# An attention and Fourier kernel whose planner leaves one PSUM bank free: scores borrow banks only while one stays, and the order's keys are spaced anew

## The chip, the cores and the metric

The kernel runs on one core of one Trainium2 chip. The metric is the time of one execution in device microseconds (us). Of the kernel before there are three timed runs, of which the median counts, and one more execution under the profiler.

## The reference, cut to what matters

Two sublayers over 2048 tokens of width 448, with their outputs side by side in one array of 2048 x 896:

```
a = einsum("bsd,ed->bse", x, dft_hid_re);  b = einsum("bsd,ed->bse", x, dft_hid_im)
y = einsum("ts,bse->bte", dft_seq_re, a) - einsum("ts,bse->bte", dft_seq_im, b)      # A: Fourier mixing
...
q, k, v = the 16 heads of x @ wqkv, 28 wide each                                        # B: attention
p = softmax(einsum("bhqd,bhkd->bhqk", q, k) * 28 ** -0.5)
out = concat_heads(einsum("bhqk,bhkd->bhqd", p, v)) @ wo
return concatenate([y, out], axis=-1)
```

All inputs and outputs are fp32.

## The kernel before, in words

**The numbers.** TensorE (PE in the profile) takes its operands as fp32r. To keep precision, most operands are split into a high part (a copy, by ScalarE) and a low part (the rest, by VectorE), and a product is a sum of two or three matmuls: high by high, low by high, high by low.

**The two kinds of PE work.** The first is attention, in `head_once` (line 1156) and `score` (line 1127). For each of 16 heads there are 16 tiles of 128 keys and 4 chunks of 512 queries, so 64 scores, 1024 in all. A *score* is one matmul at L1130 of 85 rows (the split operands and a row with the maximum to subtract) into one bank of PSUM. ScalarE (ACT) reads the bank, takes the exponential and writes it to a tile `kept` in SBUF (L1134); then the bank is free again. After 16 scores a *weighting* follows (`four`, L1141): 16 products of the exponentials by the values, 32 columns wide and four side by side, each recorded as two matmuls. There are 64 weightings. Behind each head (for the last head, behind each chunk) `normal` (line 1188) copies the sums out (L1194), sends them through DRAM to form reciprocals and stores the head's output to `on_d`.

The second kind is called *fill* here, since it stands in the order wherever scores leave room: the projections to q, k and v and the transform over the width (helper `chain`, L571), the transform over the tokens with its rows halved by symmetry (`sequence_halved`, L901, with matmuls of 448 or 226 columns), one middle row (L849), and the output projection (`project_late`: L1364, and its last rows L1395). Fill chains accumulate into one bank over 9 to 12 matmuls or, in `sequence_halved`, over a chunk of many. A few small matmuls (L1114) find the maxima of 32 keys per head (`tops`).

**The banks of PSUM.** There are eight. Four (`fill_s`, in the order's names bank_270 to bank_273) are for fill, four (`bank_s`, bank_274 to bank_277) for scores, weightings and `tops`. The pool of the scores has the pool of fill as its lender: when none of its own is free, it takes one of the lender's (line 381, and `Slots.can_take` and `Slots.take`, lines 117 to 130).

**What sets the order.** Every instruction is a task with a key. `Schedule.run` plays the tasks through on guessed durations: for each engine it takes, among the tasks that are ready and whose buffers are free, the one with the smallest key; the sequence that comes out is what each engine's queue gets. On the chip each engine then runs its queue strictly in that order, and waits by semaphores where something isn't there yet. Fill gets its keys by `fkey` (line 470), spaced evenly up to `T_FILL`; head h's scores start at `T_ATT + h * (T_END - T_ATT) / H` (line 455) and follow each other at `DT`; the output rows' last step has keys from `T_OUT`. The numbers are the planner's microseconds, and only their order counts. A weighting goes first when PE has just done one and another is ready, and it is preferred by its key otherwise.

A second path, for inputs whose checks (`flag`, L1423) fail, lies behind a branch and isn't executed in the profile.

Of the kernel before, what the change touches and what calls it, by code (L numbers as in the profile page):

```python
# [35 lines left out]
NQS = 8  # L36
NQB = 1
NFILL = 4
NQ = 4
QT = NT // NQ  # L40
Q_YO = 2
# [57 lines left out]
class Slots:  # L99
# [17 lines left out]
    def can_take(self, slots, before):  # L117
        n = sum(since <= before for _, since in self.free)
        if self.lender:
            n += sum(since <= before for _, since in self.lender.free)  # L120
        if n < len(slots) + max(s.spare for s in slots):
            return False
        if self.in_turn:
            return all(s in self.turns[:n] for s in slots)
        return True
# [187 lines left out]
def tile_kernel(ctx, tc, xa, wre, wim, wd, xb, wqkv, wo, out):  # L313
# [8 lines left out]
    def new(name, shape, dtype=F32, n=None, in_turn=False):  # L322
        if n is None:
            return sb.tile(shape, dtype, tag=name, name=name)
        sch.pools.append(Slots([sb.tile(shape, dtype, tag=f"{name}{i}", name=f"{name}{i}") for i in range(n)], in_turn))
        return sch.pools[-1]
# [10 lines left out]
    mid_d = dram.tile([1, D], F32, name="midd")  # L337
    far_d = [dram.tile([P, D], F32, name=f"fard{n}") for n in range(2 * NQ)]

# [23 lines left out]
    ones = new("ones", [P, 1])  # L363
    diff = new("diff", [P, 2 * NQ + 1, 3 * QT + 1])
    whole = new("whole", [P, 2 * NQ + 1])
    alike = new("alike", [P, 2, 2 * NQ + 1])
    edge = new("edge", [P, 4, NT])
# [12 lines left out]
    sch.pools.append(raw_s)  # L380
    fill_s, bank_s = Slots(banks[:NFILL]), Slots(banks[NFILL:])
    bank_s.lender = fill_s
# [5 lines left out]
    nc.gpsimd.memset(diff[:, :, 3 * QT:], 0.0)  # L388
    nc.gpsimd.memset(diff[:, 2 * NQ, 4:3 * QT], 0.0)
    nc.vector.tensor_tensor(fold, ident[:, :VW], ident[:, VW:2 * VW], op=ALU.add)  # L390
# [47 lines left out]
            nc.vector.tensor_copy(dst, src)  # L438


    T_ATT, T_END, T_FILL, T_OUT = 34.0, 755.0, 824.0, 766.0
    units = [(h, c) for h in range(H - 1) for c in range(NC)] + [(H - 1, c) for c in LAST]
    due, head_due, head_due_b = {}, {}, {}

# [578 lines left out]
    before = {}  # L1023
# [462 lines left out]
```

## Time and profile before

| | |
|---|---|
| median of three runs | 865.23 us (864.64 to 870.12) |
| the profiled execution, its own time | 868.95 us |
| its span, first to last instruction | 866.7 us |
| granted TensorE clock, mean over the span | 0.98 |
| PE busy, matmuls | 843.5 us, 97% of the span |
| ScalarE busy | 634.9 us, 73% |
| VectorE busy | 375.6 us, 43% |
| first score, last score start (trace) | 65 us, 825 us |

How to read it: "PE" rows are matmuls, "PEld" the loads of their stationary operand, which overlap. A row's start is when the matmul was taken up, and its duration reaches to its modelled end. Since matmuls overlap in the pipeline, the time that one costs is the distance from its start to the next start, not its duration, and PE counts as busy while it in fact waits a fraction of a microsecond between two of them. The timeline merges neighbours of one kind: "x16" is sixteen in a row. In the table by windows each engine has its busy time and the number of its instructions, followed by the granted clock (1.00 is full), the share of the DMA engines and GB/s.

### The profile page before, as it was taken

What the parts mean: (1) busy time and instruction counts of PE and PEld (TensorE: products, weight loads), DVE (VectorE), ACT (ScalarE), POOL (GpSimd) and SP (SyncE); (2) the same over time, 40 slices, a digit from 0 to 9 for tenths busy, and PEclk for the clock granted to TensorE, in tenths of its full rate; (3) what the DMA queues carried; (4) which work ended last, traced back from release to release, by engine and by line L of the source; (5) the groups of instructions that cost most, each with busy time, mean ns of one, the idle gap of its engine ahead of it and who ended that gap; (6) DMA issues with size and microseconds to landing.
All of it is one profiled execution on the core that took longest, in us unless ns stands there. A gap on an engine that the chain in (4) does not pass through costs nothing.

```text
span 866.7 us, 14119 instructions
## 1 busy us (share of the span) xinstructions
PE 843.5 (97%) x4856; PEld 532.5 (61%) x4856; DVE 375.6 (43%) x888; ACT 634.9 (73%) x1287; POOL 6.0 (1%) x27
## 2 busy tenths in 40 slices
PE   8988999999999999999999999999999999999896
PEld 7875455556555556666556655667566656666575
DVE  7541013111311132222379463667766575756341
ACT  6107787787877878878899766789887876788831
POOL 2000000000000000000000000000000000000000
PEclk9998999999999999999989999999899999999999
DMA  9867634424343454434597664558886653746433
GB/s 285 207 113 192 193 116 123 158 90 133 100 152 111 127 155 122 132 112 142 172 219 220 204 189 137 179 171 246 192 250 208 191 171 119 224 144 175 125 117 106
DMA packets 156239, 141.27 MB, mean 163 GB/s; under 512 B 69310, under 2 KB 125120, under 8 KB 156160
## 3 DMA queue, kind: packets, MB, share of 16 engines
q1 hardware_dynamic: 156160, 140.29, 54.9%
q8 instruction: 40, 0.66, 0.3%
q14 instruction: 39, 0.32, 0.1%
HBM read 98.82 MB, written 43.12 MB: 164 GB/s over the span
## 4 chain that ended last, share of the span: by engine, by line
PE 86%; ACT 5%; DMA 4%; DVE 2%; SPq 1%; issue 1%; ACTq 0%; DVEq 0%
PE bank L1130 27%; PE bank L1141 25%; PE bank L571 18%; PE bank L901 10%; ACT kept L1134 3%; PE bank L1364 3%; DMA wraw<-wre 1%; PE bank L849 1%; DMA kept<-ond 1%; DMA qb<-qkd 1%; PE bank L1114 1%; DMA kept<-xb 1%; PE bank L1395 1%; DMA v<-vd 1%; PE bank L1221 1%
## 5 line engine op out<-in xcount | busy, mean ns | idle before, releaser
L1134 ACT ACTIVATE kept<-bank 128x512 f32<-128x512 f32 x1024 | 522.9, 669 | 104.6 <-PE bank L1130 103.6
L1130 PE MATMUL bank<-q,k 85*128 85x512 f32 x1024 | 345.4, 416 | 7.2 <-ACT kept L1134 3.7
L1130 PEld LDWEIGHTS bank<-q,k 85*128 85x128 f32 x1024 | 184.2, 190 | 104.9 <-ACT kept L1134 50.5
L1141 PE MATMUL bank<-kept,v 128*32 128x512 f32 x2048 | 236.3, 602 | 0.9 <-DMA v<-vd 0.9
L1141 PEld LDWEIGHTS bank<-kept,v 128*32 128x32 f32 x2048 | 60.6, 111 | 136.1 <-issue 131.4
L901 PE MATMUL bank<-big,wlo 128*128 128x226 f32 x512 | 96.9, 285 | 0.0
L901 PEld LDWEIGHTS bank<-big,wlo 128*128 128x128 f32 x512 | 85.7, 202 | 15.1 <-issue 7.5
L571 PE MATMUL bank<-big,whi 128*128 128x512 f32 (+1 forms) x260 | 93.3, 397 | 1.3 <-DVE big L432 1.0
L901 PE MATMUL bank<-big,whi 128*128 128x448 f32 (+1 forms) x256 | 74.7, 338 | 0.2 <-ACT kept L1134 0.2
L873 DVE TENSOR_REDUCE diff<-wlo 128x1 f32<-128x512 f32 x96 | 65.6, 683 | 2.5
L571 PEld LDWEIGHTS bank<-big,whi 128*128 128x128 f32 x260 | 48.5, 190 | 16.3 <-issue 2.8
L901 PEld LDWEIGHTS bank<-big,whi 128*128 128x128 f32 x256 | 50.9, 208 | 7.6 <-ACT kept L1134 2.2
L891 DVE TENSOR_TENSOR wlo<-wraw,whi 128x512 fp32r<-128x512 f32 x32 | 22.0, 688 | 62.9 <-PE bank L901 49.5
L613 DVE TENSOR_TENSOR wd<-bank,wd 128x512 fp32r<-128x512 f32 x16 | 11.1, 691 | 82.9 <-ACT wd L612 82.9
L571 PE MATMUL bank<-big,wlo 128*128 128x512 f32 x112 | 44.6, 400 | 0.0
L571 PE MATMUL bank<-wd,whi 128*128 128x450 f32 (+1 forms) x128 | 43.0, 376 | 0.0
L438 DVE COPY kept<-bank 128x450 f32<-128x450 f32 (+2 forms) x31 | 19.3, 622 | 54.4 <-PE bank L571 54.0
L546 DVE TENSOR_TENSOR wlo<-wraw,whi 128x384 fp32r<-128x384 f32 x23 | 12.8, 556 | 69.2 <-ACT whi L542 60.7
L612 ACT ACTIVATE wd<-bank 128x512 fp32r<-128x512 f32 x16 | 10.8, 676 | 42.2 <-PE bank L571 42.2
L571 PE MATMUL bank<-wd,big 128*128 128x448 f32 x176 | 38.3, 376 | 0.0
L571 PEld LDWEIGHTS bank<-wd,big 128*128 128x128 f32 x176 | 33.9, 194 | 3.9 <-issue 0.9
L1364 PE MATMUL bank<-big 128*128 128x448 f32 x144 | 33.0, 368 | 0.0
(117 smaller groups left out, 588.6 us busy)
## 6 DMA issues: line engine op xcount, KB each, us to landing
wdraw<-wre SPq DMA_DIRECT2D x48, 256.0 KB
wdraw<-wim SPq DMA_DIRECT2D x48, 256.0 KB
qkd<-wd SPq DMA_DIRECT2D x32, 256.0 KB
q<-qkd SPq DMA_DIRECT2D x64, 112.0 KB
k<-qkd SPq DMA_DIRECT2D x64, 112.0 KB
abd<-kept SPq DMA_DIRECT2D x16, 448.0 KB
kept<-abd SPq DMA_DIRECT2D x16, 448.0 KB
qkd<-kept SPq DMA_DIRECT2D x24, 256.0 KB
```

Of the source, the lines that this page charges most:

```text
L438: nc.vector.tensor_copy(dst, src)
L546: b = dve(at, lambda: nc.vector.tensor_tensor(self.lo.t[:, :n], raw.t[:, :n], f32(self.hi.t)[:, :n], op=ALU.subtract), 0.15 * n, deps=[a], ...
L571: nc.tensor.matmul(o.t[:, :cols], w(), x(), start=(i == 0), stop=(i == n - 1))
L612: a = act(key, lambda o=o, hi=hi: nc.scalar.activation(as_r(hi.t), o.t, AF.Copy), deps=[end], use=[o, *own])
L613: b = dve(key, lambda o=o, hi=hi, lo=lo: nc.vector.tensor_tensor(as_r(lo.t), o.t, as_f(hi.t), op=ALU.subtract), deps=[a], use=[o, *own])
L873: seen.append(dve(key, lambda: nc.vector.tensor_reduce(dst, f32(flat(src.t)), axis=AX.X, op=ALU.max, apply_absolute_value=True), 0.6, deps ...
L891: b = dve_on(key - 11.5, lambda e: e.tensor_tensor(turned(lo.t), read(same.t), f32(turned(hi.t)), op=ALU.subtract), 0.65, deps=[a], acq=[l ...
L901: nc.tensor.matmul(o.t[:, at0:at0 + n], cut_of(w.t, e, c), x(), start=first, stop=stop)
L1130: m = pe(key, lambda e: nc.tensor.matmul(b.t, KT[h][kt // 4].t[:KR + 1, kt % 4 * P:(kt % 4 + 1) * P], q.t[:KR + 1, :], start=True, stop=True),
L1134: return act(key - 20, lambda: nc.scalar.activation(p.t, b.t, AF.Exp, scale=SCALE), deps=[m], use=[b, pair])
L1141: nc.tensor.matmul(o.t[j * VW:(j + 1) * VW, :], VT[h].t[:, kt // 4, kt % 4, :], tiles[i // 2].t[:, i % 2, :], start=(kt < 4 // len(cs)), s ...
L1364: nc.tensor.matmul(o.t[:, :D], a(), b(), start=(i == 0), stop=(i == 8 and n < N_HELD))
```

## The change

`can_take` no longer counts all of the lender's free banks, but all but one (`LEFT = 1`). So a score may borrow a bank of fill's only while another one of the four stays free. And the keys are spaced anew: the heads' keys run from 32 to 729 in place of 34 to 755 (a head's share is 43.6 in place of 45.1), fill's keys end at 830 in place of 824, and the last step of the output starts at 794 in place of 766. The number of instructions of each kind is the same. Since one line is added near the top, a line below it is numbered one higher after the change.

```diff
@@ constants @@
 NFILL = 4
+LEFT = 1
 NQ = 4
...
@@ Slots.can_take @@
         n = sum(since <= before for _, since in self.free)
         if self.lender:
-            n += sum(since <= before for _, since in self.lender.free)
+            n += max(0, sum(since <= before for _, since in self.lender.free) - LEFT)
         if n < len(slots) + max(s.spare for s in slots):
             return False
...
@@ keys @@
-    T_ATT, T_END, T_FILL, T_OUT = 34.0, 755.0, 824.0, 766.0
+    T_ATT, T_END, T_FILL, T_OUT = 32.0, 729.0, 830.0, 794.0
```

Since both edits act through the planner, what changes is the order. Two places show it.

**PE, in head 0, behind the third weighting.** Before, the rows between this weighting and the next are sixteen scores and nothing else; the first twelve stand here (q and k are the score's operands, the number of a bank tells which one it writes):

```order
L1130 MATMUL bank_275<-q_227,k_221 128x512
L1130 MATMUL bank_276<-q_228,k_221 128x512
L1130 MATMUL bank_277<-q_225,k_221 128x512
L1130 MATMUL bank_274<-q_226,k_221 128x512
L1130 MATMUL bank_272<-q_227,k_221 128x512
L1130 MATMUL bank_275<-q_228,k_221 128x512
L1130 MATMUL bank_273<-q_225,k_221 128x512
L1130 MATMUL bank_276<-q_226,k_221 128x512
L1130 MATMUL bank_270<-q_227,k_221 128x512
L1130 MATMUL bank_277<-q_228,k_221 128x512
L1130 MATMUL bank_274<-q_229,k_222 128x512
L1130 MATMUL bank_272<-q_230,k_222 128x512
```

No fill stands among them, and three of fill's banks (270, 272, 273) hold scores. After the change the same place begins so (L1131 is the score, L572 a fill matmul of a projection):

```order
L1131 MATMUL bank_274<-q_228,k_221 128x512
L1131 MATMUL bank_275<-q_225,k_221 128x512
L1131 MATMUL bank_276<-q_226,k_221 128x512
L1131 MATMUL bank_277<-q_227,k_221 128x512
L1131 MATMUL bank_271<-q_228,k_221 128x512
L572 MATMUL bank_270<-big,whi_213 128x512
L1131 MATMUL bank_274<-q_225,k_221 128x512
L572 MATMUL bank_270<-big,wlo_216 128x512
L1131 MATMUL bank_275<-q_226,k_221 128x512
L572 MATMUL bank_270<-big,whi_213 128x512
L1131 MATMUL bank_276<-q_227,k_221 128x512
```

It goes on in the same way: behind the first five scores they alternate one by one, up to the next weighting seventeen scores and thirteen fill matmuls, these into bank 270 and at last 273. Over the whole program the scores stand in 461 unbroken runs before, five of them 11 to 16 long, and in 716 after, none longer than 9; 351 runs before and 607 after are a single score.

**ACT, near the end, where it prepares the last operands of the output projection.** Before, the six copies of the second half of the heads' outputs (L1349; `kept` has been loaded from `on_d`) stand ahead of the last 13 exponentials (L1134):

```order
L1134 ACTIVATE kept_243<-bank_275 128x512
L1349 ACTIVATE big<-kept_248 128x512 x2
L1349 ACTIVATE big<-kept_237 128x512
L1349 ACTIVATE big<-kept_253 128x512
L436 ACTIVATE kept_241<-bank_277 128x512
L1134 ACTIVATE kept_243<-bank_276 128x512
L1134 ACTIVATE kept_244<-bank_274 128x512
```

After the change (L1135 is the exponential, L1350 the copy) they stand behind the last exponential:

```order
L1135 ACTIVATE kept_241<-bank_275 128x512
L1135 ACTIVATE kept_241<-bank_273 128x512
L437 ACTIVATE wdraw<-bank_272 128x448
L1350 ACTIVATE big<-kept_253 128x512 x2
L437 ACTIVATE kept_243<-bank_277 128x512
L1350 ACTIVATE big<-kept_244 128x512 x2
L1350 ACTIVATE big<-kept_242 128x512
L1195 ACTIVATE kept_251,sums<-bank_276 32x512
```

No exponential follows these copies any more. The six copies of the first half, of which three stood 41 or 42 and three 30 exponentials ahead of the end before, now stand together 13 exponentials ahead of it.

## The prediction, on record before the run

> **What bounds the kernel now.** I read the page first: which engine is full, and through what the chain that ended last runs.
>
> ```profile
> span 866.7 us, 14119 instructions
> PE 843.5 (97%) x4856; PEld 532.5 (61%) x4856; DVE 375.6 (43%) x888; ACT 634.9 (73%) x1287; POOL 6.0 (1%) x27
> ...
> PE 86%; ACT 5%; DMA 4%; DVE 2%; SPq 1%; issue 1%; ACTq 0%; DVEq 0%
> PE bank L1130 27%; PE bank L1141 25%; PE bank L571 18%; PE bank L901 10%; ACT kept L1134 3%; PE bank L1364 3%; DMA wraw<-wre 1%; PE bank L849 1%; DMA kept<-ond 1%; DMA qb<-qkd 1%; PE bank L1114 1%; DMA kept<-xb 1%; PE bank L1395 1%; DMA v<-vd 1%; PE bank L1221 1%
> ```
>
> PE sets the time. The change leaves its instructions as they are, so it can only win what PE loses between them. The 97% hides that loss, since a matmul counts as busy while it waits. So I count: instructions times the distance from start to start, for the stretch with the scores, 60 to 825 us. The table by windows gives its length and the granted clock, the groups of PE in that window the counts.
>
> ```profile
> 60.00:825.00 765.00, 755.42 (x4442) 459.24 (x4441) 328.54 (x771) 606.63 (x1238) 1.28 (x4) 0.98 0.54 162
> ...
> 82.00:89.00 7.00, 6.08 (x33) 1.53 (x32) 0.69 (x1) 3.51 (x8) 0.00 (x0) 0.53 0.66 207
> 443.00:450.00 7.00, 7.00 (x23) 5.48 (x24) 6.15 (x17) 7.00 (x17) 0.00 (x0) 0.54 0.98 307
> 614.00:621.00 7.00, 6.82 (x25) 4.38 (x27) 3.12 (x11) 5.56 (x13) 0.00 (x0) 0.51 0.81 94
> 713.00:717.00 4.00, 4.00 (x20) 2.89 (x22) 0.36 (x2) 3.68 (x8) 0.00 (x0) 0.57 0.55 168
> 819.00:823.00 4.00, 4.00 (x9) 2.05 (x8) 0.99 (x2) 3.53 (x8) 0.00 (x0) 0.58 0.08 27
> ```
>
> ```profile
> L1130 PE MATMUL bank<-q,k 85*128 85x512 f32 x1023 | 345.1, 416 | 7.2 <-ACT kept L1134 3.7 <-ACT kept L436 2.2 <-DMA q<-md 0.9
> L1141 PE MATMUL bank<-kept,v 128*32 128x512 f32 x2016 | 232.7, 602 | 0.9 <-DMA v<-vd 0.9
> L901 PE MATMUL bank<-big,wlo 128*128 128x226 f32 x512 | 96.9, 285 | 0.0
> L571 PE MATMUL bank<-big,whi 128*128 128x512 f32 x168 | 59.5, 403 | 0.0
> L901 PE MATMUL bank<-big,whi 128*128 128x448 f32 x128 | 50.8, 397 | 0.2 <-ACT kept L1134 0.2
> L571 PE MATMUL bank<-big,wlo 128*128 128x512 f32 x96 | 38.5, 401 | 0.0
> L901 PE MATMUL bank<-big,whi 128*128 128x226 f32 x128 | 35.8, 280 | 0.0
> ```
>
> The distances come from the timeline of PE, at a place where nothing waits (536 to 544 us, then two fill matmuls of 512 columns):
>
> ```profile
> 536.16 3.64 PE L1141 MATMUL bank<-kept,v 128*32 128x512 f32 x32
> 539.73 0.38 PE L901 MATMUL bank<-big,whi 128*128 128x226 f32 x1
> ...
> 543.32 0.40 PE L1130 MATMUL bank<-q,k 85*128 85x512 f32 x1
> 543.55 0.27 PE L901 MATMUL bank<-big,whi 128*128 128x226 f32 x1
> 543.66 0.28 PE L901 MATMUL bank<-big,wlo 128*128 128x226 f32 x1
> 543.78 0.41 PE L1130 MATMUL bank<-q,k 85*128 85x512 f32 x1
> 544.02 0.37 PE L901 MATMUL bank<-big,whi 128*128 128x448 f32 x1
> 544.23 0.39 PE L1130 MATMUL bank<-q,k 85*128 85x512 f32 x1
> ...
> 189.92 0.39 PE L571 MATMUL bank<-big,wlo 128*128 128x512 f32 x1
> 190.15 0.40 PE L571 MATMUL bank<-big,whi 128*128 128x512 f32 x1
> ```
>
> A weighting costs 3.57 us (32 records; 2016 are 63 of them), a score 0.23 to 0.24, say 0.236, fill of 226 columns 0.11 to 0.12, of 448 columns 0.21, of 512 columns 0.23. So: 1023 x 0.236 = 241.4; 63 x 3.57 = 224.9; 640 x 0.115 = 73.6; 128 x 0.21 = 26.9; 264 x 0.233 = 61.5; the remaining 371 of the 4442, nearly all 450 columns or fewer, at 0.2 = 74.2. Together 702.5 us of 765. **62.5 us are lost.** Of these the lowered clock takes 7 x 0.47 + 7 x 0.46 + 7 x 0.49 + 4 x 0.43 + 4 x 0.42 = 13.3 us. **About 49 us are waits** of PE, some 6 of them at the entries of the weightings (0.1 us each), which stay.
>
> Where are they? The timeline shows it best in head 0, at the very place of the order shown above, PE first and then ACT:
>
> ```profile
> 95.36 5.67 PE L1130 MATMUL bank<-q,k 85*128 85x512 f32 x16
> 100.96 3.64 PE L1141 MATMUL bank<-kept,v 128*32 128x512 f32 x32
> 104.53 5.67 PE L1130 MATMUL bank<-q,k 85*128 85x512 f32 x16
> 110.13 2.35 PE L1141 MATMUL bank<-kept,v 128*32 128x512 f32 x20
> ```
>
> ```profile
> 95.96 7.95 ACT L1134 ACTIVATE kept<-bank 128x512 f32<-128x512 f32 x16 [1.45 <-PE bank L1130]
> ```
>
> Sixteen scores take 110.13 - 104.53 = 5.60 us in place of 16 x 0.236 = 3.78: 1.82 us of waiting. ACT takes (7.95 - 0.67) / 15 = 0.485 us an exponential, twice PE's 0.236; once all banks in reach are full, PE goes at ACT's pace, for there is no fill between the scores. The list of waits has it over the whole span, with PE's weight load as the one that waits (it overlaps work, so the sum is an upper bound):
>
> ```profile
> PEld bank L1130 <- ACT kept L1134: 50.5, 182, 1.6
> ```
>
> **The change part by part.** *Removed and added:* no instruction. *Moved:* fill. One free bank of fill's stays out of the scores' reach, so a new fill chain always finds one, and the planner can put a fill matmul where it would have nothing but the next score.
>
> What this is worth at the place shown: the changed order has 17 scores and 13 fill matmuls between the third weighting and the fourth. PE's work is 3.57 + 17 x 0.236 + 13 x 0.233 = 10.6 us. Does a score wait? Count from the first score's start. The row above has the first exponential 0.60 us behind it (95.36 to 95.96); the next follow each 0.48 us, and a bank is free 0.67 us (mean of L1134 on the page) and some 0.05 after its exponential's start. The first five scores start at 0, 0.24, 0.47, 0.71, 0.94. Then a fill and a score alternate, 0.47 us a pair. Bank 274 is wanted again at 1.41 and free at 0.60 + 0.72 = 1.32; bank 275 at 1.88 and 1.80; bank 276 at 2.35 and 2.28; bank 277 at 2.82 and 2.76; on the next round 274 at 3.76 and 3.72. No wait, with a few hundredths to spare: a pair (0.47) goes at ACT's own pace. So where the order before lost 1.82 us in 9.17, the changed one loses about nothing in 10.6.
>
> The place at 536 to 548 shows that this pattern holds on the chip, since there the order before already alternates: 71 PE and 17 ACT instructions in 10 us, without a gap.
>
> ```profile
> 538.00:548.00 10.00, 10.00 (x71) 7.84 (x63) 6.54 (x17) 7.86 (x17) 0.00 (x0) 1.00 0.43 132
> ```
>
> *What remains.* There are 64 groups, one to a weighting. I put 54 ordinary ones at 0.2 us: above the nothing of the arithmetic, since a margin of hundredths is used up by any late exponential. The other ten are the last two and those where ACT also prepares the transform's operands, 6 to 12 other operations in a group against 1 to 3 elsewhere by the order, each near 0.5 us: there I leave 0.8 us each. With the weightings' 6 this makes 11 + 8 + 6 = 25 us in place of 49: **24 us less.** The bounds: nothing but the entries remains (6: 43 less), or all waits stay, since they come from ACT and not from the banks (0 less).
>
> *The clock.* The five half-rate stretches each stand behind a place where PE had waited: of the 8 us ahead of the last one, PE was busy in 5.8.
>
> ```profile
> 811.00:819.00 8.00, 5.77 (x41) 2.13 (x40) 4.10 (x7) 5.72 (x12) 0.00 (x0) 1.00 0.44 158
> ```
>
> With half the waits some of them go; I take one or two of five, **3 us less**, with bounds of 13 less (none left) and 13 more (twice as many).
>
> *The near end.* That wait at 811 to 819 is of another kind. A load from DRAM is late, ACT's copies wait for it, and the 13 exponentials queued behind them wait too, and so do PE's scores. Chain, then ACT:
>
> ```profile
> 808.78 7.42 DMA kept<-ond
> ```
>
> ```profile
> 814.97 0.63 ACT L1349 ACTIVATE big<-kept 128x512 fp32r<-128x512 f32 x1 [1.66 <-DMA kept<-ond]
> 816.22 1.67 ACT L1349 ACTIVATE big<-kept 128x512 fp32r<-128x512 f32 x3 [0.62 <-DMA kept<-ond]
> ```
>
> In the changed order these copies stand behind the last exponential, and those of the first half take their place. Their loads now stand in SP's queue behind the sums and stores of head 14, and two of the three behind the read of the first chunk's reciprocals; if that read is late, the same 13 exponentials wait for it. So I count nothing extra here: the 2.3 us are in the sum above. Other queues are covered: POOL has four instructions in the window, VectorE is at 328.5 of 765 us, and projections are done long ahead of their heads in both orders.
>
> *Outside of the window* nothing changes that I can see: up to the first scores the order is nearly the same, and behind the last weighting's sum stand 117 fill matmuls in place of 92, which cover the last head's way through DRAM.
>
> *Sum:* 24 + 3 = 27 us, so a span of 866.7 - 27 = 839.7 and 868.95 - 27 = 842 for the profiled execution. That one lies 3.7 us above the median of the runs, with which the result will be compared: 865.2 - 27 = **838 us.**
>
> [...]
>
> **The rivals.** *A: the banks were not what was short.* PE's waits come from ACT being late (loads, copies in its queue); fill between the scores then only moves them, and 49 us become some 43. For it: ACT is at 606.6 of 765 us, and the place near 815. Against it: the sixteen in a row, with nothing ahead of them on ACT but exponentials. The time would be 865 - 6 = 859.
>
> *B: too few banks, slower.* With four own banks and fewer loans, each other operation of ACT (167 between the 17th and the 1010th score by the changed order) stands in front of an exponential whose bank is wanted at once: every margin above is under 0.1 us, and such an operation takes 0.5. If half of them delayed PE in full, 167 x 0.5 x 0.5 = 42 us of waits would come on top of the 25, 67 in all against 49: 18 more, 883 us. It decides from about 100 delays of 0.5 us. Against it: during each weighting (3.57 us) the three or four scores ahead keep ACT only some 2 us busy, so it has 1.5 us for other operations; and the changed order puts three and more fill matmuls between two scores at such places.
>
> *C: nearly all waits go,* and with them the lowered clock: 40 + 10 = 50 us less, 815. For it: the arithmetic above gives no wait at all. Against it: the late loads stay, and the groups with many operations on ACT.
>
> *D: the clock follows the alternation* and not the waits: twice as many half-rate stretches, 13 us more than now, so 865 - 24 + 13 = 854. Against it: 538 to 548 alternates at a clock of 1.00. [...]
>
> **How the numbers follow.** The forecast gets 0.66, A 0.12, B 0.06, C 0.10, D 0.06. What a measurement can tell from no change is about 1%, 8.7 us, so from 856.6 to 873.9 counts as the same. Faster are the forecast, C and D: 0.82; the same is A: 0.12; slower is B: 0.06. The forecast's own range reaches from 828 (waits 14 us, clock as now less 3) to 850 (waits 36, clock as now). For 8 in 10 it reaches to D on the one side and into C on the other: 822 to 857.
>
> **What would show it.** In the profile after, the scores' groups in head 0 should alternate with L572 matmuls and end without a run at 0.35 us a score; the wait of L1131's weight load for L1135 should fall from 50.5 us to under 30; PE's distances in the window of the scores should leave 30 to 45 us over the counted work in place of 62.5; ACT's busy time should stay at 635. It is wrong if the counted loss stays at 60 (A), if waits of scores for ACT grow in number beyond the 182 and in sum beyond 60 (B), or if half-rate stretches become more than seven (D).

## The result and the profile after

The changed kernel takes **837.0 us** (median of four runs, 835.5 to 842.7), the kernel before in the same comparison 867.7 us. The ratio is 0.964, with a 95% interval of 0.955 to 0.973. The profiled execution has a span of 840.4 us in place of 866.7, and its own time, 842.68 us, is the longest of the four. The forecast was 838 us and a span of 839.7. The kernel before was 2.4 us slower in this comparison than in the runs that the forecast started from, so the medians fall by 30.7 us where 27 were forecast; the profiled pair falls by 26.3.

The page, in the order in which it was read before: the full engine, then the chain.

```profile
span 840.4 us, 14124 instructions
...
PE 820.5 (98%) x4856; PEld 536.0 (64%) x4856; DVE 384.0 (46%) x900; ACT 623.0 (74%) x1275; POOL 6.0 (1%) x27
...
PE 91%; ACT 3%; DMA 3%; SPq 1%; DVE 1%; issue 0%; ACTq 0%
```

PE still sets the time, with as many instructions as before. Its share of the chain rose from 86% to 91%: ScalarE's and the transfers' parts of it shrank. ScalarE's busy time fell from 634.9 to 623.0 us; the section on the prediction comes back to that.

The place in head 0 that the prediction worked out, behind the third weighting, in the timeline of PE:

```profile
105.58 3.64 PE L1142 MATMUL bank<-kept,v 128*32 128x512 f32 x32
109.15 1.43 PE L1131 MATMUL bank<-q,k 85*128 85x512 f32 x5
110.42 0.40 PE L572 MATMUL bank<-big,whi 128*128 128x512 f32 x1
110.65 0.40 PE L1131 MATMUL bank<-q,k 85*128 85x512 f32 x1
...
115.86 0.43 PE L1131 MATMUL bank<-q,k 85*128 85x512 f32 x1
116.13 0.40 PE L572 MATMUL bank<-big,wlo 128*128 128x512 f32 x1
116.46 3.64 PE L1142 MATMUL bank<-kept,v 128*32 128x512 f32 x32
```

From weighting to weighting it is 116.46 - 105.58 = 10.88 us, where the arithmetic without any wait gave 10.6. Of the 0.28 us between them, about 0.1 is the entry of the weighting. Before, this place lost 1.82 us.

The list of waits has for the whole span, with the weight load of the scores as the one that waits:

```profile
PEld bank L1131 <- ACT kept L1135: 26.6, 91, 3.3
```

It was 50.5 us in 182 waits. Now the account of lost time, as the prediction made it. The table by windows has the length of the stretch with the scores, the number of PE's instructions and the two stretches at half rate that are left in it; the groups of PE in the window 60 to 830 have the counts (four of the rows stand here).

```profile
60.00:830.00 770.00, 763.37 (x4611) 487.90 (x4610) 351.51 (x814) 603.19 (x1242) 1.28 (x4) 0.99 0.55 166
82.00:89.00 7.00, 6.83 (x20) 4.20 (x24) 0.61 (x1) 5.61 (x12) 0.20 (x1) 0.51 0.82 257
451.00:458.00 7.00, 6.59 (x24) 5.99 (x25) 5.75 (x16) 5.00 (x11) 0.00 (x0) 0.53 0.98 292
```

```profile
L1131 PE MATMUL bank<-q,k 85*128 85x512 f32 x1024 | 373.5, 412 | 5.7 <-ACT kept L1135 4.2 <-DVE wd L614 1.0 <-DMA k<-qkd 0.5
L1142 PE MATMUL bank<-kept,v 128*32 128x512 f32 x2048 | 233.6, 597 | 0.0
L902 PE MATMUL bank<-big,wlo 128*128 128x226 f32 x512 | 106.3, 280 | 0.0
L572 PE MATMUL bank<-big,whi 128*128 128x512 f32 x168 | 65.1, 402 | 0.0
```

With the prediction's prices: 1024 x 0.236 + 64 x 3.57 + 640 x 0.115 + 128 x 0.21 + 264 x 0.233 + 507 others x 0.2 = 733.6 us of 770. So 36.4 us are lost in place of 62.5. The clock has 7 x 0.49 + 7 x 0.47 = 6.7 of them (13.3 before), waits the other 29.7 (49 before), entries of weightings included. The two falls, 6.6 and 19.5, make 26.1 us; the span fell by 26.3.

Near the end, the timeline of ScalarE shows the copies L1350 of the first half among the last exponentials:

```profile
778.91 6.32 ACT L1135 ACTIVATE kept<-bank 128x512 f32<-128x512 f32 x13
785.12 3.22 ACT L1350 ACTIVATE big<-kept 128x512 fp32r<-128x512 f32 x6
...
791.24 4.87 ACT L1135 ACTIVATE kept<-bank 128x512 f32<-128x512 f32 x10
```

No copy waits for its load there, and the exponentials behind start at once. What still waits is elsewhere, at 441 to 452 us. There ScalarE's queue has copies (L785) of a load from DRAM ahead of exponentials, and PE's next score stands behind them. ScalarE first, then PE:

```profile
445.52 0.68 ACT L785 ACTIVATE big<-kept 128x226 fp32r<-128x226 f32 x2 [2.90 <-DMA kept<-abd]
...
448.66 0.67 ACT L785 ACTIVATE big<-kept 128x226 fp32r<-128x226 f32 x2 [1.36 <-DMA kept<-abd]
```

```profile
451.41 0.79 PE L1131 MATMUL bank<-q,k 85*128 85x512 f32 x1 [2.98 <-ACT kept L1135]
```

The half-rate stretch near 451 to 458 begins at 450.75 us in the trace's record of the clock, in the last part of this wait.

### The profile page after: what moved, and what is told of

It is laid out like the page before. It is cut to its first block, busy times and chain, and to the rows that moved or that the text cites. A ratio compares the mean times of both kernels' runs of the same rounds, so it can differ in the third digit from the quotient of the medians.

```text
span 840.4 us, 14124 instructions
## 1 busy us (share of the span) xinstructions
PE 820.5 (98%) x4856; PEld 536.0 (64%) x4856; DVE 384.0 (46%) x900; ACT 623.0 (74%) x1275; POOL 6.0 (1%) x27
## 4 chain that ended last, share of the span: by engine, by line
PE 91%; ACT 3%; DMA 3%; SPq 1%; DVE 1%; issue 0%; ACTq 0%
PE bank L1131 30%; PE bank L1142 26%; PE bank L572 18%; PE bank L902 11%; PE bank L1365 4%; ACT kept L1135 2%; PE bank L850 1%; PE bank L1115 1%; DMA kept<-abd 1%; DMA kept<-xb 1%; PE bank L1396 1%; PE bank L1222 0%; ACT big L790 0%; DMA vd<-kept 0%; DMA qb<-qkd 0%
## 5 line engine op out<-in xcount | busy, mean ns | idle before, releaser
L1135 ACT ACTIVATE kept<-bank 128x512 f32<-128x512 f32 x1024 | 513.2, 669 | 137.6 <-PE bank L1131 137.1
L1131 PE MATMUL bank<-q,k 85*128 85x512 f32 x1024 | 373.5, 412 | 5.7 <-ACT kept L1135 4.2
L1131 PEld LDWEIGHTS bank<-q,k 85*128 85x128 f32 x1024 | 187.4, 190 | 103.3 <-issue 40.7
L1142 PE MATMUL bank<-kept,v 128*32 128x512 f32 x2048 | 233.6, 597 | 0.0
L902 PE MATMUL bank<-big,wlo 128*128 128x226 f32 x512 | 106.3, 280 | 0.0
L902 PEld LDWEIGHTS bank<-big,wlo 128*128 128x128 f32 x512 | 96.4, 201 | 9.0 <-issue 0.2
L572 PE MATMUL bank<-big,whi 128*128 128x512 f32 (+1 forms) x260 | 99.0, 396 | 1.6 <-DVE big L433 1.0
L902 PE MATMUL bank<-big,whi 128*128 128x448 f32 (+1 forms) x256 | 75.8, 325 | 0.9 <-DVE big L791 0.9
L439 DVE COPY kept<-bank 128x450 f32<-128x450 f32 (+2 forms) x46 | 28.6, 621 | 78.4 <-PE bank L572 74.9
L572 PEld LDWEIGHTS bank<-big,whi 128*128 128x128 f32 x260 | 49.9, 193 | 11.8 <-DVE big L433 1.7
L902 PEld LDWEIGHTS bank<-big,whi 128*128 128x128 f32 x256 | 49.8, 199 | 5.7 <-DVE big L791 1.2
L614 DVE TENSOR_TENSOR wd<-bank,wd 128x512 fp32r<-128x512 f32 x16 | 10.9, 690 | 89.9 <-ACT wd L613 89.9
L572 PE MATMUL bank<-big,wlo 128*128 128x512 f32 x112 | 44.6, 400 | 0.0
L572 PE MATMUL bank<-wd,whi 128*128 128x450 f32 (+1 forms) x128 | 41.8, 367 | 0.0
L572 PE MATMUL bank<-wd,big 128*128 128x448 f32 x176 | 40.3, 389 | 0.0
L572 PEld LDWEIGHTS bank<-wd,big 128*128 128x128 f32 x176 | 35.2, 201 | 4.5 <-issue 0.9
L1118 DVE STREAM_TRANSPOSE kept<-bank 128x512 f32<-128x512 f32 (+1 forms) x20 | 14.2, 712 | 35.7 <-PE bank L1115 35.7
L1195 ACT ACTIVATE kept<-bank 128x512 f32<-128x512 f32 (+1 forms) x19 | 11.4, 600 | 24.4 <-PE bank L1142 24.4
```

Source lines behind the costliest of these rows:

```text
L572: nc.tensor.matmul(o.t[:, :cols], w(), x(), start=(i == 0), stop=(i == n - 1))
L614: b = dve(key, lambda o=o, hi=hi, lo=lo: nc.vector.tensor_tensor(as_r(lo.t), o.t, as_f(hi.t), op=ALU.subtract), deps=[a], use=[o, *own])
L902: nc.tensor.matmul(o.t[:, at0:at0 + n], cut_of(w.t, e, c), x(), start=first, stop=stop)
L1118: r = dve(key, lambda o=o, mt=mt: nc.vector.transpose(mt.t[:32 * n, 0], o.t[:32 * n]), 0.64, deps=[m], acq=[mt], use=[o], own=RAW_S)
L1131: m = pe(key, lambda e: nc.tensor.matmul(b.t, KT[h][kt // 4].t[:KR + 1, kt % 4 * P:(kt % 4 + 1) * P], q.t[:KR + 1, :], start=True, stop=True),
L1135: return act(key - 20, lambda: nc.scalar.activation(p.t, b.t, AF.Exp, scale=SCALE), deps=[m], use=[b, pair])
```

## The experiments

So that the runs can be compared, each profiled span was split in three: PE's waits, its clock, and the rest. Clock is half of the half-rate time up to PE's last matmul (in the stretch from 614.16 us before, at a granted clock of 0.50, it is 0.40 us from the start of a matmul of 448 columns to the next start, elsewhere 0.21). Waits are the distances from start to start of PE's matmuls, less what was counted as clock in them and less the distance that the same form needs where nothing waits, above 0.08 us, without the weightings' entries, over the whole span. The rest comes out between 797 and 801 us in every run, so the split takes in nearly all of the difference. The profiled execution is one of the runs and not the median one: that of the changed kernel is the slowest of its four, that of e1 the fastest, that of e4 the slowest of ten. So medians tell how long a kernel takes, and the split tells where a time goes. (Before and after, its waits are not those of the account above, since it has the start in it and not the entries.)

| kernel | median, us | ratio to before (95%) | span | waits | clock | rest |
|---|---|---|---|---|---|---|
| before | 867.7 | | 866.7 | 52.8 | 15.4 | 798.5 |
| changed | 837.0 | 0.964 (0.955 to 0.973) | 840.4 | 30.4 | 10.2 | 799.8 |
| e1: bank left, old keys | 844.9 | 0.978 (0.971 to 0.986) | 840.0 | 35.0 | 5.1 | 799.9 |
| e2: new keys alone | 884.6 | 1.023 (1.016 to 1.029) | 879.2 | 64.2 | 17.1 | 797.9 |
| e3: two banks left | 849.0 | 0.982 (0.975 to 0.989) | 846.8 | 34.6 | 11.9 | 800.3 |
| e4: no loans | 871.2 | 1.006 (1.003 to 1.010) | 874.7 | 51.7 | 24.6 | 798.4 |
| e5: before, half exponentials | 847.1, one run | | 845.4 | 34.7 | 13.7 | 797.0 |
| e6: changed, half exponentials | 826.9, one run | | 825.1 | 22.7 | 3.4 | 799.0 |
| e7: changed, three late exponentials | 859.7, one run | | 857.4 | 43.1 | 15.4 | 798.9 |
| e8: changed again | 837.0 | 0.965 (0.962 to 0.968) | 834.8 | 30.5 | 5.1 | 799.2 |
| e9: e1 again | 845.8 | 0.975 (0.973 to 0.978) | 841.5 | 36.9 | 5.1 | 799.5 |
| e10: other keys | 834.1 | 0.963 (0.960 to 0.967) | 831.8 | 27.1 | 5.1 | 799.6 |
| e11: loads allowed for | 838.2 | 0.966 (0.964 to 0.969) | 838.4 | 34.1 | 3.4 | 800.9 |

e1 to e4 ran on one chip, e5 to e7 on a second, e8 to e11 on a third, each beside the kernel before, whose median was 866.6 and 867.8 us on the first and the third and whose one run on the second took 863.9. The ratios are to the kernel before on the same chip; for e1 to e7, differences to the changed kernel are between separate comparisons.

### One half of the change alone: e1 and e2

```diff
# e1: LEFT = 1, and the keys of before
-    T_ATT, T_END, T_FILL, T_OUT = 32.0, 729.0, 830.0, 794.0
+    T_ATT, T_END, T_FILL, T_OUT = 34.0, 755.0, 824.0, 766.0
# e2: the new keys, and all free banks may be borrowed
-LEFT = 1
+LEFT = 0
```

> One free bank is kept (LEFT = 1), the keys are those of before. Theory (the bank): PE's waits go because fill stands between the scores, which the order shows with the old keys too (687 runs of scores, 577 of them a single score, against 461 and 351 before). Then most of the gain is here: 837 + 6 = 843 us, between 838 and 850; the loss over the counted work in the window of the scores falls from 62 us to about 40. Rival (the keys): the gain comes from the heads' earlier keys, which leave more fill behind the last score; then 858 or more.

> The new keys with all of fill's banks on loan (LEFT = 0). The order has 439 runs of scores, 30 of them of 10 to 20, against 461 and 19 before; the last score stands 9 us of PE work earlier than before, since more fill is left for the end. Theory (the bank): the runs wait at the pace of the exponentials as before, so 860 to 872, no gain; perhaps up to 4 us less for what the earlier last score covers. Rival (the keys): 845 or less.

The bank alone brings 21.8 us (844.9 against 866.6). Its wait of scores for exponentials has the same sum as in the changed kernel:

```profile
PEld bank L1131 <- ACT kept L1135: 26.6, 107, 1.0
```

The new keys alone cost 18 us: 884.6, well above what was expected of them. The timelines of PE and the table by windows of e2 show how:

```profile
172.29 7.52 PE L1131 MATMUL bank<-q,k 85*128 85x512 f32 x20
179.75 5.96 PE L1142 MATMUL bank<-kept,v 128*32 128x512 f32 x32
```

```profile
157.00:173.00 16.00, 16.00 (x73) 12.90 (x70) 6.54 (x13) 5.19 (x11) 0.00 (x0) 1.00 0.81 271
173.00:187.00 14.00, 14.00 (x56) 5.50 (x55) 0.69 (x1) 10.72 (x23) 0.00 (x0) 0.76 0.31 93
```

From 157 to 173 us PE runs nearly nothing but fill, and ScalarE is busy in 5.19 of 16 us. Then twenty scores come in one run, into own and borrowed banks, and with no fill among them PE goes at ScalarE's pace: 7.46 us to the next weighting where 20 x 0.236 = 4.72 would do. The clock falls at 177.65 us, still within this run of scores, and the weighting takes 5.89 us instead of 3.57. e2 has 30 runs of ten or more scores, before 19, the changed kernel none. So the heads' closer keys alone make the bunching worse, and only the bank that is left makes them useful.

### How many banks: e3 and e4

```diff
-LEFT = 1
+LEFT = 2      # e3;  e4: 4, which forbids every loan
```

> New keys, two free banks kept. Theory: one free bank is enough to start a chain of fill, the second only takes loans from the scores. By the order 776 runs, but before a weighting only 2.5 scores of the next group are issued in place of 3.1, so that during the 3.6 us of a weighting the exponentials run dry 0.3 us earlier, 64 times: 15 to 20 us lost, 850 to 857. Rival (the more alternation, the better): 832 or less.

> New keys, no loans at all: scores have their four banks alone. The slow rival of the prediction in its pure form. Theory: only 2.3 scores are issued ahead of a weighting, and half of the scores find their bank used again within 1.3 us of PE work, where turn-around takes 1.2 to 1.3: waits come back, 865 to 880, slower than before or equal to it. If loans mattered little: 840 to 850.

Two banks left cost 12 us against one, and no loans at all cost 34 (849.0 and 871.2 against 837.0). Both directions were as expected (e3 1 us below its range), but not for the reason that the expectations and rival B gave, short margins at each weighting. Between 100 and 350 us neither e3 nor e4 waits more than the changed kernel; by the rule of the split all three lose 2 to 3 us there, and the kernel before 11. e4 loses at few places. Here is PE near the end, first the timeline, then the window of e4 and that of the changed kernel:

```profile
750.32 5.12 PE L1142 MATMUL bank<-kept,v 128*32 128x512 f32 x32
755.37 0.96 PE L1131 MATMUL bank<-q,k 85*128 85x512 f32 x3
756.55 6.19 PE L1131 MATMUL bank<-q,k 85*128 85x512 f32 x12 [0.22 <-ACT kept L1135]
762.68 5.77 PE L1142 MATMUL bank<-kept,v 128*32 128x512 f32 x32
```

```profile
740.00:790.00 50.00, 49.55 (x207) 21.75 (x203) 10.83 (x23) 34.98 (x72) 0.00 (x0) 0.83 0.35 106
```

```profile
740.00:790.00 50.00, 50.00 (x317) 30.77 (x309) 30.85 (x76) 42.51 (x89) 0.47 (x1) 1.00 0.50 151
```

In 50 us e4 gets through 207 instructions, the changed kernel through 317. The fill of the transform is used up in e4 (6 matmuls of L902 after 740 us, against 96 in the changed kernel), while 126 scores are still to come, against 78. They then run bare, at ScalarE's pace, and the clock is low for much of the stretch, 0.83 in its mean. Without loans the scores fall behind the fill, and the cover is spent too early. Two more places add to it, both with late data: a score waits behind ScalarE's copies of a late load at 392 us, and PE waits for the last operands of the output. e3 has a milder form of the first: after 740 us 93 scores and 51 matmuls of L902 are left, and eight scores in a row from 743.59 us take 4.16 us. How much of its 12 us each place has was not worked out. The two late loads of e4, from ScalarE's timeline, then PE's:

```profile
388.55 0.67 ACT L785 ACTIVATE big<-kept 128x226 fp32r<-128x226 f32 x2 [3.85 <-DMA kept<-abd]
```

```profile
392.44 0.79 PE L1131 MATMUL bank<-q,k 85*128 85x512 f32 x1 [4.23 <-ACT kept L1135]
...
864.58 3.35 PE L1396 MATMUL bank<-big,q 128*128 128x448 f32 x8 [7.24 <-DVE q L1386]
```

### Is it ScalarE's pace? e5 and e6

```diff
-        return act(key - 20, lambda: nc.scalar.activation(p.t, b.t, AF.Exp, scale=SCALE), ...)
+        return act(key - 20, lambda: nc.scalar.activation(p.t[:, :CH // 2], b.t[:, :CH // 2], AF.Exp, scale=SCALE), ...)
```

e5 does this to the kernel before, e6 to the changed one; each keeps its own order. The exponentials of the second half of each chunk of queries are left out (their tiles are zeroed once at the start), the reciprocals are replaced by zeros, and the checks' branch is not taken, so the attention half of the output is zero.

> The kernel before with its order unchanged, but each exponential does only the first 256 of its 512 columns (the other half of the tiles is filled with zeros once, at the start, the reciprocals of the sums are replaced by zeros and the check of the inputs is left out, so the attention half of the output is not computed). An exponential should take about 0.27 us in place of 0.48, near a score's 0.236. Theory (the order's runs go at the pace of the exponentials): the sixteen in a row take about 4.3 us in place of 5.6, PE's waits in the window of the scores fall from 49 to below 20 us and the lowered clock with them; the span falls by 30 us or more, to 835 or less, apart from up to 10 us more at the start. Rival A of the prediction (late loads, ACT's queue): waits stay at 40.

> The same halved exponentials in the changed order. Theory: little is left to gain from ACT's pace, since fill already stands where PE would wait: the span falls by 5 to 15 us from 840, and both orders come within 10 us of each other. If the changed order were still held at ACT's pace, it would fall by 25 or more.

In e5 a run of sixteen scores now costs next to nothing more than sixteen scores. PE:

```profile
93.15 3.93 PE L1132 MATMUL bank<-q,k 85*128 85x512 f32 x16
97.00 3.64 PE L1143 MATMUL bank<-kept,v 128*32 128x512 f32 x32
```

3.85 us to the weighting, against 5.60 before and 3.78 without a wait. So it was ScalarE's pace that held these scores. The waits of the scores' weight loads for exponentials all but vanish in both, from 50.5 to 4.2 us and from 26.6 to 6.0. The span of e5 falls by 21.3 us against the profile before and that of e6 by 15.3 against the profile after; beside the one run of the kernel before on the same chip, e5 is 16.7 us shorter.

Three things were expected and did not come: a fall of 30 us or more in e5, waits below 20 us there (34.7 are left), and that the two orders would be within 10 us of each other. e5 is still 20.3 us behind e6, 12 of it waits and 10 clock. The list of waits of e5 shows what it waits for instead:

```profile
PEld bank L1116 <- DMA qb<-qkd: 5.8, 3, 2.7
PEld bank L1132 <- ACT kept L1136: 4.2, 8, 2.0
PEld bank L903 <- DVE wlo L930: 3.5, 3, 2.5
PEld bank L573 <- ACT whi L544: 2.3, 1, 2.3
PEld bank L1132 <- ACT kept L438: 2.1, 1, 2.1
```

Single operands that come late, each some 2 us at a time. Once the exponentials no longer hold PE, it reaches these places sooner. Whether the order before would have met them at its own speed can't be read from this pair, since its order was planned for full exponentials. So the pair shows that ScalarE's pace held the runs of scores, and leaves open how much of the change's 22 us of waits is owed to that alone.

### Does the clock follow waits? e7

Three single exponentials of the changed kernel, in heads 3, 5 and 7, are issued 5, 9 and 17 times over (the same values again), at places where PE otherwise runs at full clock without a wait.

```diff
+TIMES = {(3, 6, 0): 5, (5, 6, 0): 9, (7, 6, 0): 17}
-        return act(key - 20, lambda: nc.scalar.activation(p.t, b.t, AF.Exp, scale=SCALE), ...)
+        def exps(n=TIMES.get((h, kt, c), 1)):
+            for _ in range(n):
+                nc.scalar.activation(p.t, b.t, AF.Exp, scale=SCALE)
+        return act(key - 20, exps, ...)
```

> The changed kernel with three exponentials repeated in place: 5 times in head 3, 9 times in head 5, 17 times in head 7, so 1.9, 3.8 and 7.7 us of extra work on ACT at three places where nothing waited and the clock was full; nothing is left out. Theory (the clock falls behind waits of PE): behind the second and the third, where PE runs out of banks and fill in the meantime for 2 us and more, a half-rate stretch of 3.4 or 6.8 us; behind the first, which the next weighting's slack takes up, none. The span rises by about 1 + 3 + 6 us of waiting and 3 to 7 us of clock. Rival D (the clock goes by alternation, or falls by chance): no low stretch at these places.

The three waits of PE in its timeline, and the half-rate stretches in the table by windows; its last row is the time ahead of the first wait:

```profile
218.49 0.50 PE L1132 MATMUL bank<-q,k 85*128 85x512 f32 x1 [2.15 <-ACT kept L1138]
...
309.60 0.80 PE L1132 MATMUL bank<-q,k 85*128 85x512 f32 x1 [4.09 <-ACT kept L1138]
...
410.50 0.80 PE L1132 MATMUL bank<-q,k 85*128 85x512 f32 x1 [9.22 <-ACT kept L1138]
```

```profile
219.00:222.40 3.40, 3.40 (x10) 2.62 (x10) 0.00 (x0) 3.25 (x7) 0.00 (x0) 0.56 0.20 70
308.00:314.80 6.80, 5.20 (x13) 4.06 (x13) 0.50 (x1) 6.63 (x14) 0.00 (x0) 0.51 0.10 30
404.00:414.20 10.20, 3.70 (x10) 3.13 (x11) 0.52 (x1) 9.88 (x20) 0.00 (x0) 0.51 0.01 1
200.00:219.00 19.00, 16.85 (x97) 10.09 (x90) 10.45 (x25) 17.82 (x37) 0.00 (x0) 1.00 0.45 144
```

With the wait of 2.15 us come 3.4 us at half rate, with that of 4.09 come 6.8, with that of 9.22 come 10.2; ahead of the first the clock was full. The second and the third stretch begin while PE still waits, at 308.18 and 403.75 us. The changed kernel has full clock at all three places:

```profile
215.00:225.00 10.00, 10.00 (x60) 5.94 (x56) 6.06 (x11) 9.94 (x22) 0.00 (x0) 1.00 0.29 99
300.00:315.00 15.00, 15.00 (x101) 8.40 (x90) 6.37 (x13) 11.12 (x23) 0.00 (x0) 1.00 0.47 138
395.00:415.00 20.00, 20.00 (x122) 12.26 (x121) 4.04 (x7) 15.50 (x32) 0.00 (x0) 1.00 0.37 125
```

So PE's waiting can lower the clock, even 2 us of it, which was not expected of the shortest. That one is paid nearly twice: 2.15 us, and 1.7 more for the 3.4 us at half rate. The longer ones cost less in proportion, since part of their half-rate time falls into the wait itself: behind 309.60 us 5.4 us of it are left, which cost 2.7, and behind 410.50 us 3.5, which cost 1.7. Not every wait of 2 us does this; the last section has two that did not. The span is 17 us longer than in the profile after; it is a single run from another comparison.

### Bank with and without the keys, measured closely, and other keys: e8 to e11

e8 is the changed kernel, e9 is e1, both run more often on one chip. e10 has keys of another choice with the bank left. e11 tells the planner to expect the late load of 441 to 452 us 3 us later, and takes the keys that suit the order that follows.

```diff
# e10
-    T_ATT, T_END, T_FILL, T_OUT = 32.0, 729.0, 830.0, 794.0
+    T_ATT, T_END, T_FILL, T_OUT = 38.0, 733.0, 832.0, 792.0
# e11
+    T_ATT, T_END, T_FILL, T_OUT = 33.0, 728.0, 822.0, 790.0
...
-                      size=448, deps=[ab_done[g], ab_done[g + HT], *after(g)], use=[x])
+                      size=448, extra=3.0, deps=[ab_done[g], ab_done[g + HT], *after(g)], use=[x])
```

> The changed kernel itself, beside the next three on the same chip. 835 to 843.

> One free bank kept, old keys, once more beside the changed kernel: do the new keys add anything? Theory: the bank gives nearly all; the keys give what the earlier last score and the copies behind the last exponential save, 2 to 8 us: 842 to 848. If the keys gave nothing, it would lie within 2 us of the changed kernel.

> One free bank kept and a third set of keys (38, 733, 832, 792 in place of 32, 729, 830, 794); 744 runs of scores. Theory: with the bank kept, keys near these are worth the same: within 4 us of the changed kernel. If the exact keys mattered, it would be 8 us or more apart.

> The changed kernel with 3 more of the planner's microseconds for the loads of the transform's operands (kept from abd), for which ACT, and behind it the exponentials and PE, waited at 445 to 451 us (4 us, and a half-rate stretch of 6.8 us behind it), and with keys near the changed ones (33, 728, 822, 790). Theory (what is left are late loads at ACT's queue, and clock behind them): 4 us of waits and 3 us of clock less, 828 to 834. Rival (the wait only moves to another late load): 835 to 843.

With the bank left, the new keys bring 8.7 us more (837.0 against 845.8), and the intervals of the two ratios don't touch. In the profiled pair 6.4 of it are waits. One such place in e9, near the end where its keys leave no fill between the scores:

```profile
747.77 4.42 PE L1131 MATMUL bank<-q,k 85*128 85x512 f32 x9
```

Nine scores take 4.35 us to the weighting in place of 2.1. Two more are waits of 1.4 and 2.5 us for the maxima's operands, at 511 and 689 us. The keys of e10 come to 834.1 us, the fastest of the versions run, but its interval overlaps that of the changed kernel; among keys near the new ones the exact choice matters little once a bank is left. e11 gains nothing (838.2): in place of the wait at 448 us stand others, of 2.5 us at 442 and 1.9 us at 493. Moving a late load in the plan moved the wait.

## Why the prediction was right

**The mechanism.** Scores without fill between them go at ScalarE's pace (sixteen in 5.60 us in head 0 before, where 3.78 do without a wait), and a bank kept back lets fill in between. Head 0 shows it to 0.28 us in 10.9, e5 shows that ScalarE's pace was the brake on such runs, and e1 shows that the bank alone takes the wait of scores for exponentials from 50.5 to 26.6 us.

**The waits.** Forecast 24 us less, measured 19.5 by the same account (49 to 29.7) and 22.4 by starts (52.8 to 30.4). The term was a little too large because of single places and not of the ordinary groups. Of the 63 groups between one weighting and the next, 43 lose less than 0.2 us with the entry, where 0.3 was put; but the load near 445 us alone has 2.83 and 1.07 us, more than the 0.8 us left for such a group.

**The clock.** Forecast 3 us less, measured 6.6 by the window's account. The step that was mis-sized is "I take one or two of five": three of the five went. The stretches at 614, 713 and 819 are gone with their waits, those near 82 and 445 remain with theirs. In e8, the same kernel profiled again, the one near 82 is missing and one near 55 us is half as long (clock 5.1 us in place of 10.2), and its span of 834.8 us is shorter by about that. So in the profiled pair the sum came out right as two errors of 4 us that cancel, which is luck; the fall of the medians, 30.7 us, is 4 more than forecast, and with e8's clock the term was 7 us short.

**The near end.** It was counted at nothing extra, and indeed the copies of the first half don't wait. The part outside of the window added nothing either: the span less the lost time of the window is 866.7 - 62.5 = 804.2 us before and 840.4 - 36.4 = 804.0 after.

**ScalarE's busy time** should have stayed at 635 and is 623. That step was wrong. Some copies that empty PSUM banks may go to ScalarE or to VectorE, as the planner finds one free, and in the new order it gave fewer to ScalarE. So the number of PE's instructions is the same, but not that of ScalarE's (1275 in place of 1287) and VectorE's. Of ScalarE's groups, before and after:

```profile
L436 ACT ACTIVATE kept<-bank 128x446 f32<-128x446 f32 (+3 forms) x23 | 13.4, 585 | 13.3 <-PE bank L1141 6.0 <-PE bank L1364 4.2 <-PE bank L571 3.0
```

```profile
L437 ACT ACTIVATE kept<-bank 128x448 f32<-128x448 f32 (+1 forms) x8 | 4.8, 601 | 9.3 <-PE bank L1142 6.0 <-PE bank L1365 3.2
```

Fifteen such copies left ScalarE, three of another tile came to it; VectorE has 900 instructions in place of 888. These 12 copies were not forecast. At 0.6 us each they are some 7 of the 12 us; most of the rest is no work saved, since busy time counts overlapping instructions once and ScalarE's overlap by 217 us in place of 213. What part of the 20 us of waits the fewer copies saved was not tried apart.

**What the prediction didn't split.** It put the whole gain on the change as one thing. The halves alone are -22 and +18 us, and together -31: the keys' sign depends on the bank.

**The rivals.** A (banks weren't short) is refuted by e1: one number about banks, with the old keys, brings 22 us. B (too few banks) has its side of the optimum, two banks left and more (e3, e4), but not by its mechanism. C put the clock at 10 us less, as far off as the forecast's 3 in the profiled pair and right for e8, yet waits of 30 us stayed. D (the clock follows the alternation) is refuted by e7 and by 100 to 125 us, where scores and fill alternate behind the first few scores of each group:

```profile
100.00:125.00 25.00, 25.00 (x140) 15.11 (x139) 3.06 (x7) 22.06 (x46) 0.00 (x0) 1.00 0.62 198
```

All eight banks are in use in each of these kernels. Giving the scores four banks only (e4) costs 34 us against the changed kernel, and giving them all eight (e2, with the same keys) costs 48; the best split of those tried leaves one bank for the other stream to start in.

**The working.** The bounds of the forecast's own range follow from its conditions as 827 and 852 us, and not as 828 and 850. Rival B loses from 48 delays of 0.5 us on by its own prices (49 - 25 = 24 us), and not from about 100. No conclusion hangs on either.

## What to carry to other kernels

Where two kinds of work share an in-order engine and a pool of buffers, and one of them is held back by a slower consumer, keep one buffer out of its reach, so that the other kind can always be put between. Judge the spacing of an order only together with that limit: the same keys cost 18 us without it and brought 9 with it. And look at the clock behind a wait of PE: in e7 the half rate behind the waits of 2.15, 4.09 and 9.22 us cost another 1.7, 2.7 and 1.7 us, while behind waits of 2.5 us in e9 and e11 the clock stayed full.

## What the runs showed of the hardware

The half-rate stretches in the traces' records of the granted clock are 3.41, 6.83 or 10.24 us long, but for the one in which a span ends. Before, those of 3.41 us begin at 54.38, 713.15 and 818.96 us, those of 6.83 at 81.68, 443.50 and 614.16; after, three of 6.83 us begin at 54.81, 82.11 and 450.75. The third of e7 is one of 10.24 us. Some waits of PE and runs of scores, and the clock behind them:

| run | at, us | what PE did | granted clock behind it |
|---|---|---|---|
| e7 | 218.49 | a wait of 2.15 us ended | half rate for 3.4 us (0.56 from 219.0 to 222.4) |
| before | 818.43 | a wait of 2.23 us ended | half rate for 3.41 us from 818.96 |
| before | 711.26 | a wait of 1.25 us ended | half rate for 3.41 us from 713.15 |
| before | 484.05 | a wait of 1.02 us ended | full clock (1.00 from 484 to 614) |
| e9 | 689 | a wait of 2.5 us | full clock |
| e11 | 442 | a wait of 2.5 us | full clock |
| e2 | 172.29 to 179.75 | twenty scores, 0.37 us apart | half rate from 177.65, within the run |
| before | 104.53 to 110.13 | sixteen scores, 0.35 us apart | full clock (1.00 from 104.5 to 110.2) |

So a wait of 2.15 us cost clock in e7, and 2.5 us in e9 and in e11 did not; in e2 the half rate came within a run of scores, without any single gap as long as 2 us. The length of a wait alone doesn't tell, and what does was not shown: no run was made to test it.
